# Thresholds of a planned instruction order, chosen by stretch, in an attention and MLP block

## The chip, the cores and the metric

The kernel runs on one core of one Trainium2 chip. The metric is the device time of one execution in microseconds; lower is better. The kernel before was timed in three runs: 2409.73, 2412.84 and 2415.67 us, a median of 2412.84. One more execution was taken with the hardware profiler on, and all rows of the profile come from that one.

The names of the engines are those of the profile: PE is TensorE's matmul, PEld its weight load, DVE VectorE, ACT ScalarE, POOL GpSimd and SP the engine that issues most transfers.

## The reference

A transformer block in f32 for 2048 rows of 576 features: layer norm with scale and shift from a condition vector, attention with 32 heads of 18 features, then a second norm and an MLP of width 4608.

```python
mod = (_silu(c) @ w_mod).reshape(c.shape[0], 6, 1, -1)
sa, ca, ga, sb, cb, gb = ...                       # the six parts of mod
h = _layernorm(x) * (1 + ca) + sa
qkv = (h @ wqkv).reshape(B, S, 3, 32, 18) ...
scores = einsum("bhqd,bhkd->bhqk", q, k) * 18 ** -0.5
o = einsum("bhqk,bhkd->bhqd", softmax(scores), v)
x = x + ga * (o @ wo)
h = _layernorm(x) * (1 + cb) + sb
out = x + gb * (silu(h @ w1) @ w2)
```

## The kernel before

**Tiling.** Queries are cut into four blocks of 512 (`NQB`), heads into eight groups of four (`NQUAD`), so there are 32 units of work for the attention. Keys are cut into 16 tiles of 128. Operands of the projections and of the MLP are split into a high and a low part in the type f32r, and a product is three passes of TensorE over those parts.

**Row scores and scores.** For each unit the kernel first needs the largest score of each query row, so that the exponential doesn't overflow. `slot_a` computes the scores with queries on the partitions (tile `psa`, L802) and takes the row maximum of each 512 on VectorE (`mx`, L804). Forty steps later (`LEAD`), `slot_b` computes the same scores with keys on the partitions (tile `psb`, L852), with the maximum already subtracted, and ScalarE writes the exponential (`pt`, L854). One value of the counter `now` is one `slot_a` and one `slot_b`; two values are one step of row scores. There are 2128 values of `now`; the first 80 are worked off in the first part, before the planned loop starts. The exponentials of a key tile for four heads are ready after four values of `now`, and then `run_pv` multiplies one or more key tiles with the values (tile `psv`, L889): four matmuls a key tile, side by side in four column strips of 32.

**Filling.** Between these, TensorE works off a list of other work (`Filler`): first the query and key projections that are still missing (`qk_one`, L591, full height of 128 rows), then, once the list is empty, the pools for the MLP are opened (`open_mlp`) and the list holds, for the block of queries that has just ended (`post`), the output projection (`psp`), the second norm, the transposes (`h_T`) and the MLP (`mlp1`, `mlp2`; tile `ps`, L486). While those run, the scores of the next block run beside them. After the last block, nothing but its own `post` is left (L480). Scores and most of the MLP use two halves of 64 rows side by side, which the planner calls mode "half"; values are mode "values"; matmuls over all 128 rows are mode "full".

**The planner.** The order of TensorE's instructions is written out in Python when the kernel is built. `Plan` holds a clock `t`, in ns, and what it believes of VectorE and ScalarE: a queue of operations for each with durations (`TMAX` 605 for a row maximum, `TEXP` 495 for an exponential) and rings of PSUM banks that come free when the operation that reads them is done. `Plan.work` moves the clock on by the price of a piece of TensorE work and adds a charge where the mode changes. The prices are `TS` (one value of `now`), `TV` (one key tile of values), `MMC` and `MMH` (a step of 512 or 288 columns of the filling work) and `TX` (a change of mode).

**The choice.** The loop at the end of `tile_adaln_block` picks, at each turn, one of three things: scores ("s"), a piece of the filling work ("f") or values ("v"); where none is possible, the planner's clock moves on by 20 ns with no instruction issued. `scores` says that the banks for one more step are free by the planner's clock and that an exponential's tile is free; `n` counts the key tiles whose exponentials are ready; `ahead` says how many values of `now` the scores are ahead of the pace at which the filling work would be finished in time; `plan.backlog("V")` is the work that waits for VectorE. Nine numbers decide between them:

- `AHEAD`: how far scores may run ahead of the filling work, and filling work ahead of scores
- `KEEP` and `NEAR`: after `open_mlp`, filling work goes first while it is less than `KEEP` values behind the scores' pace and the next point at which it must wait is at most `NEAR` ns off
- `LOADED`: before `open_mlp`, values go first if VectorE has at least so many ns of backlog for each key tile that is ready
- `LOADED2` and `NEXT`: before `open_mlp`, when TensorE is not in mode "half", filling work goes first if VectorE has at least `LOADED2` ns of backlog and the filling work is not more than `NEXT` values ahead
- `STAND`: how long the planner stands before it takes fewer key tiles than it would like
- `PVMAX` and `PVMIN`: the number of ready key tiles that go at once whatever else is possible, and the number that go (after `open_mlp`) before scores where no filling work can start

Before the change each of the nine is one constant for the whole kernel. Row maxima are read by VectorE alone, and banks of `psa` form a ring of three, so where VectorE is behind, the next `psa` matmul stands in TensorE's queue, and all that is queued behind it with it.

The order of the other engines' instructions is the order in which the Python code issues them; a few transfers and conversions are tied to a place in TensorE's order by `after_pe`. The first part (`start_tasks`) has its own planner with its own durations.

Of the kernel before, what the change touches and what calls it, by code (L numbers as in the profile page):

```python
# [57 lines left out]
REST = (16, 8, 0, 0)  # L58
LP = 8000
PB = 9  # L60
PVMAX, PVMIN = 5, 3
EACH, LAND, STORE = (1500, 2000), 5000, 4000
QKB = 3
GS = 2
# [2 lines left out]
GQ = (range(0, 4), range(4, 8), range(8, 11), range(11, 14))  # L67
G2 = [range(i, i + 3) for i in range(0, 24, 3)]
GP = [range(i, i + 2) for i in range(0, 28, 2)]
MMC = 231  # L70
MMH = 133

TS, TV, TX, TL, TR = 231, 906, 95, 430, 60
TMAX, TEXP = 605, 495
TLAT = {"A": 100, "V": 85}
AHEAD = 12
KEEP = 6
NEAR = 500
LOADED = 900
LOADED2 = 900  # L80
NEXT = 8
STAND = 0


def head_rows(h):
# [14 lines left out]
class Plan:  # L100
# [11 lines left out]
    def work(self, cost, mode="half"):  # L112

        if mode != self.mode:
            cost += 2 * TX if mode == "half" else TX
            self.mode = mode
        self.t += cost

# [222 lines left out]
def tile_adaln_block(ctx: ExitStack, tc: tile.TileContext, x, wqkv, wo, w1, w2, c, wfirst, wcol, out):  # L341
# [85 lines left out]
    half = {"at": 0}  # L427
# [82 lines left out]
    full = wqp.tile([P, P], F32, name="full", bufs=1)  # L510
# [74 lines left out]
    def qk_one(which, m, n, w, part):  # L585
        if part == 0:
            qk_ps[0] = psF.tile([P, 512], F32, tag="f", name="psqk")
            qk_ps[1] = plan.take("f")
        for i in GQ[part]:
            kt, a, b = PASS[i]  # L590
            mm(qk_ps[0], lhsT=w[b][:, kt, :], rhs=(hTl if a else hTh)[:, kt, n * 512:(n + 1) * 512], start=(i == 0), stop=(i == 13))  # L591
        if part == len(GQ) - 1:

            hl, tmp = qk_hi(qk_ps[0]), qk_ps["t"].tile([P, 512], F32, name="qt")
            nc.scalar.activation(tmp, qk_ps[0], AF.Copy)
            nc.gpsimd.tensor_tensor(hl[:, 1], tmp, f(hl)[:, 0], op=ALU.subtract)
            qk_store(which, m, n, hl, (0, 1))
            chain([("A", 600), ("A", 600)], plan.t + 200, None, qk_ps[1])
# [31 lines left out]
    def add_qk(steps):  # L630
# [7 lines left out]
        for i, (which, m, pairs) in enumerate(steps):  # L638
            for n in sum(pairs, ()):
                names = [("qkx"[which], m, n)]  # L640
                for p in range(len(GQ)):
                    fill.add(MMC * len(GQ[p]), lambda i=i, which=which, m=m, n=n, p=p: qk_one(which, m, n, qk_w[i], p), name=names, need=bank_need if p == 0 else None, mode="full")
                    if p == 0 and asked:
# [310 lines left out]
    def post(b):  # L954
# [26 lines left out]
        def proj(j, part):  # L981
            if part == 0:
                def ops(g, i):
                    kt, a, w = PASS[i]
                    return (c["tl"] if a else c["th"])[:, kt, j * P:(j + 1) * P], c["wo", kt][:, 1 - w, g * HH:(g + 1) * HH]

                settle(*[("wo", kt) for kt in range(KT)])
                c["pp"] = Pair([bank("psp", psA)[:, :HH] for _ in range(2)], ops, 14, not state["tail"])
            for s in GP[part]:
                c["pp"].step(s)  # L990
            if part == len(GP) - 1:
                for g in range(2):
                    add_x1(j, g, c["pp"].ps[g])
                    plan.op("AV"[g == 0], plan.t + 200, 440, c["pp"].release[g])
# [63 lines left out]
        for j in range(NST):  # L1058
            rest(REST[j])
            steps_ = dict(zip((1, 4, 8, 11), ln_steps(j - 1))) if j else {}  # L1060
            for part in range(len(GP)):
                fl.add(MMH * len(GP[part]), lambda j=j, part=part: proj(j, part), need={0: pair_need if j else o_need, len(GP) // 2: half_need}.get(part))
                if part in steps_:
# [32 lines left out]
        def mlp1(i, part):  # L1096
            if part == 0:
                def ops(g, k):
                    if k == 14:
                        return c["w1", i + g][:, 0, 4 * P:], c["h2"]  # L1100
                    kt, a, w = PASS[k]
                    return c["w1", i + g][:, 1 - w, kt * P:(kt + 1) * P], (c["hl"] if a else c["hh"])[:, kt, :]

                settle(("w1", i), ("w1", i + 1))
                c["p1"] = Pair([bank("ps1", psA) for _ in range(2)], ops, 14, not state["tail"], short=not last)
            for s in GR[not last][part]:
                c["p1"].step(s)
            if part < NG - 1:
                return
            us = c["p1"].ps  # L1110
            if not state["tail"]:

                us = [etmp(), etmp()]
                nc.scalar.activation(us[0], c["p1"].ps[0], AF.Copy)
                nc.vector.tensor_copy(us[1], c["p1"].ps[1])
                c["gs"] = []
                for n in range(2):
                    chain([(("A", 600), ("V", 690))[n], ("A", 630), ("V", 690), ("A", 630)], plan.t + 200, c["p1"].release[n], lambda at: c["gs"].append(at + 1600))
            for g_ in range(2):
                u, t = us[g_], etmp()  # L1120
                nc.scalar.activation(t, u, AF.Tanh, scale=0.5)  # L1121
                nc.vector.scalar_tensor_tensor(t, t, 1.0, u, op0=ALU.add, op1=ALU.mult)  # L1122
                g = pool.tile([P, 2, QB], F32R, tag="g", name="g", bufs=GB)
                nc.scalar.activation(g[:, 0, :], t, AF.Copy)  # L1124
                (nc.vector if last else nc.gpsimd).tensor_tensor(g[:, 1, :], t, f(g[:, 0, :]), op=ALU.subtract)  # L1125
                c["g", i + g_] = g
# [38 lines left out]
        def w_at(n, *loads):  # L1165

            for at, load, i in loads:
                if at == n and i < NFT:
                    fl.add(0, lambda load=load, i=i: load(i))

        def add_mlp1(i, *loads):

            for part in range(NG):
                fl.add(MMC * len(GR[not last][part]), lambda part=part: mlp1(i, part), need={0: pair_need, NG // 2: half_need}.get(part))
                w_at(part, *loads)

        def add_mlp2(i0, add, *loads):
            for j in range(NST):
                for part in range(len(G2)):
                    add(MMH * len(G2[part]), lambda j=j, part=part: mlp2(i0, j, part), None, {0: pair_need, len(G2) // 2: half_need}.get(part))  # L1180
                    w_at(j * len(G2) + part, *loads)
# [375 lines left out]
    now = 2 * LEAD  # L1557
    fill.pace(now, NQUAD * 64 - END0)
    stood = 0
    while now < 2 * (total + LEAD) or pend or later:  # L1560
        plan.advance()
        if "p" not in mp and fill.pos == len(fill.items):
            open_mlp()
            prefetch(0)
        state["now"] = now
        run_later()
        serve()
        fill.free()
        more = now < 2 * (total + LEAD)
        n = kts_ready()  # L1570
        room = state["p"] + (now % 2 == 0) <= len(pts)
        scores = more and room and plan.is_ready(plan.when("b")) and (now // 2 >= total or plan.is_ready(plan.when("a")))
        work = fill.pos < len(fill.items)
        target = fill.target() if work else now + AHEAD - 1
        ahead = now - target
        busy = work and fill.ready()
        if n >= PVMAX or n and more and not room and (ahead < 0 or not busy):
            do = "v"
        elif "p" not in mp:

            if busy and plan.mode != "half" and ahead > -NEXT and plan.backlog("V") >= LOADED2:
                do = "f"
            elif scores and ahead < AHEAD:
                do = "s"
            elif n and plan.backlog("V") >= LOADED * n:
                do = "v"
            elif busy and ahead > -AHEAD:
                do = "f"
            elif scores:
                do = "s"  # L1590
            elif n and stood >= STAND:
                do = "v"
            else:
                do = None
        elif busy and (ahead >= 0 or ahead > -KEEP and fill.rest() <= NEAR):
            do = "f"
        elif n >= PVMIN and not busy:
            do = "v"
        elif scores and ahead < AHEAD:
            do = "s"  # L1600
        elif busy and ahead > -AHEAD:
            do = "f"
        elif n >= PVMIN or n and stood >= STAND:
            do = "v"
        else:
            do = None
        stood = 0 if do else stood + 20
        if not do:
            if not more and not pend:
                run_later(2)  # L1610
                state["now"] += 1
                now += 1
            plan.t += 20
            continue
        if do == "v":
            run_later(1)
            run_pv(n)
        elif do == "f":
            fill.one()
        else:  # L1620
            sa, j = divmod(now, 2)
            plan.work(TS)
            if sa < total:
                slot_a(sa, j)
            slot_b(sa - LEAD, j)
            now += 1
            plan.advance()
# [50 lines left out]
```

## Time and profile before

| what | before |
|---|---|
| median of three runs | 2412.84 us |
| profiled execution, its time | 2407.57 us |
| profiled execution, its span | 2405.8 us |
| TensorE busy | 2323.4 us, 97% |
| VectorE busy | 1775.2 us, 74% |
| ScalarE busy | 1482.1 us, 62% |
| granted TensorE clock, mean | 0.992 |

The span runs from the first to the last instruction of the program; the execution's own time is 1.8 us longer. A row of the profile's fifth part or of a list of groups has the line in the kernel, the engine, the operation, the tile written and the tiles read, the shapes and the count, then the busy time, the mean of one in ns and the idle time of the engine just before them with what ended it. A row of waits has who waited for whom, then the sum in us, the number of times and the longest. A row of a table by stretches has a stretch, its length and for each engine the busy time and the count, then the granted clock. A row of the timeline, or of the chain of waits in order of time, has a start and a length in us and then what ran.

### The profile page before, as it was taken

The page shows a single profiled execution, that of the slowest core. Times are in us where ns is not written, and L with a number is a line of the kernel's source. Part 1 is how long each engine was busy: PE and PEld are TensorE (multiplying, and loading weights), DVE is VectorE, ACT ScalarE, POOL GpSimd, SP SyncE. Part 2 cuts the span into 40 slices and gives each one's busy share as a digit, 9 for nine tenths or more (in the row PEclk, how much of TensorE's full clock was granted, in tenths as well). Part 3 has the DMA queues.
Part 4 walks back from the last instruction along what each step waited for, and adds up shares of the span by engine and source line. Part 5 has one row for each costly group of instructions (what it writes and reads, how often), then busy time and mean ns, then how long its engine had stood idle before and what let it go on. Part 6 is the DMA issues. An engine that isn't in the chain of part 4 may idle for free.

```text
span 2405.8 us, 52151 instructions
## 1 busy us (share of the span) xinstructions
PE 2323.4 (97%) x19844; PEld 1596.2 (66%) x19844; DVE 1775.2 (74%) x3109; ACT 1482.1 (62%) x2734; POOL 637.5 (26%) x769
## 2 busy tenths in 40 slices
PE   6999999998999999998999999999999999989999
PEld 4874444434567766775676777766677777678998
DVE  8768989887878888886887888887877787144333
ACT  5247777775667776675776777775676677722121
POOL 5201011104746676663311111122211111110000
PEclk9999999999999999999999999999999999999999
DMA  7555556445556666665655445554545554336563
GB/s 254 163 173 173 168 170 182 150 159 157 195 191 206 213 223 208 221 220 180 216 172 175 164 164 191 170 181 139 188 160 167 189 166 163 120 113 225 203 206 118
DMA packets 201474, 433.02 MB, mean 180 GB/s; under 512 B 31362, under 2 KB 67618, under 8 KB 201226
## 3 DMA queue, kind: packets, MB, share of 16 engines
q1 hardware_dynamic: 201226, 429.68, 54.5%
q8 instruction: 159, 2.61, 0.5%
q14 instruction: 89, 0.73, 0.1%
HBM read 338.54 MB, written 86.33 MB: 177 GB/s over the span
## 4 chain that ended last, share of the span: by engine, by line
PE 84%; DVE 7%; DMA 4%; ACT 3%; POOL 2%; issue 1%; SPq 0%; ACTq 0%; POOLq 0%; DVEq 0%
PE ps L486 25%; PE psv L889 18%; PE psa L802 13%; PE ps L480 10%; PE psb L852 8%; PE psqk L591 3%; DVE mx L804 3%; PE psp L486 2%; PE psv L486 2%; DMA raw<-in_w 1%; ACT pt L854 1%; PE psqk L486 1%; PE psv L1350 1%; PE psqk L1350 1%; PE psp L480 1%
## 5 line engine op out<-in xcount | busy, mean ns | idle before, releaser
L804 DVE TENSOR_REDUCE mx<-psa 128x1 f32<-128x512 f32 x2048 | 1319.0, 683 | 310.9 <-PE psb L852 161.8
L854 ACT ACTIVATE pt<-psb 128x512 f32<-128x512 f32 x2048 | 1131.5, 598 | 503.1 <-PE psb L852 305.8
L852 PE MATMUL psb<-qt,kb 56*128 56x512 f32 x2048 | 750.1, 423 | 10.7 <-ACT pt L854 9.7
L802 PE MATMUL psa<-ka,qt 54*128 54x512 f32 x2016 | 698.2, 415 | 9.5 <-DVE mx L804 8.0
L802 PEld LDWEIGHTS psa<-ka,qt 54*128 54x128 f32 x2016 | 335.2, 186 | 298.7 <-DVE mx L804 202.0
L889 PE MATMUL psv<-pt,vt 128*32 128x512 f32 x4096 | 513.5, 604 | 2.3 <-ACT ov L893 1.7
L486 PE MATMUL ps<-w2t,g 64*128 64x288 f32 x4992 | 410.5, 294 | 7.7 <-POOL w2t L693 3.9
L486 PEld LDWEIGHTS ps<-w2t,g 64*128 64x128 f32 x4992 | 382.7, 186 | 43.0 <-DVE mx L804 10.1
L852 PEld LDWEIGHTS psb<-qt,kb 56*128 56x128 f32 x2048 | 352.4, 185 | 53.6 <-ACT pt L854 38.4
L486 PE MATMUL ps<-hh,w1t 64*128 64x512 f32 x1944 | 371.6, 395 | 6.8 <-POOL w1t L696 3.1
L486 PEld LDWEIGHTS ps<-hh,w1t 64*128 64x128 f32 x1944 | 220.3, 186 | 44.9 <-DVE mx L804 7.5
L889 PEld LDWEIGHTS psv<-pt,vt 128*32 128x32 f32 x4096 | 99.5, 109 | 215.8 <-issue 208.0
L1125 POOL TENSOR_TENSOR g<-etmp,g 128x512 fp32r<-128x512 f32 x108 | 137.8, 1297 | 392.3 <-ACT g L1124 334.6
L1003 POOL TENSOR_TENSOR x<-x,gt 128x288 f32<-128x288 f32 x116 | 93.6, 807 | 416.9 <-ACT gt L1002 416.9
L486 PE MATMUL ps<-hl,w1t 64*128 64x512 f32 x864 | 198.0, 393 | 0.5 <-POOL hl L413 0.5
L999 DVE TENSOR_TENSOR x<-ps,x 128x288 f32<-128x288 f32 x184 | 83.8, 456 | 124.8 <-PE ps L480 77.1
L480 PE MATMUL ps<-w2t,g 128*128 128x288 f32 x960 | 133.5, 299 | 7.4 <-ACT g L1124 5.9
L480 PEld LDWEIGHTS ps<-w2t,g 128*128 128x128 f32 x960 | 131.1, 191 | 9.9 <-ACT g L1124 6.3
L486 PEld LDWEIGHTS ps<-hl,w1t 64*128 64x128 f32 x864 | 105.3, 186 | 10.8 <-POOL hl L413 0.9
L1121 ACT ACTIVATE eq<-ps 128x512 f32<-128x512 f32 x36 | 21.6, 600 | 146.3 <-PE ps L480 146.3
L480 PE MATMUL ps<-hh,w1t 128*128 128x512 f32 x360 | 106.9, 390 | 0.5 <-DVE hh L415 0.5
L1122 DVE SCALAR_TENSOR_TENSOR etmp<-etmp 128x512 f32<-128x512 f32 x108 | 76.6, 744 | 23.4 <-ACT etmp L1121 23.2
(146 smaller groups left out, 2084.4 us busy)
## 6 DMA issues: line engine op xcount, KB each, us to landing
w1t<-w1s SPq DMA_DIRECT2D x108, 640.0 KB
w2t<-w2s SPq DMA_DIRECT2D x108, 576.0 KB
kb<-kscr SPq DMA_DIRECT2D x512, 108.0 KB
ka<-kscr SPq DMA_DIRECT2D x504, 108.0 KB
w1s<-w1t SPq DMA_DIRECT2D x36, 640.0 KB
w2s<-w2t SPq DMA_DIRECT2D x36, 576.0 KB
vt<-vscr SPq DMA_DIRECT2D x32, 608.0 KB
qt<-qscr SPq DMA_DIRECT2D x128, 108.0 KB
```

The source lines that it names most:

```text
L480: mm(self.ps[late], lhsT=lhsT, rhs=rhs, start=(i == 0), stop=(i == self.n - 1))
L486: done = mm(self.ps[g], lhsT=lhsT[rows], rhs=rhs[rows], start=(s == 0), stop=(s == self.end))
L591: mm(qk_ps[0], lhsT=w[b][:, kt, :], rhs=(hTl if a else hTh)[:, kt, n * 512:(n + 1) * 512], start=(i == 0), stop=(i == 13))
L802: mm(ps, lhsT=t["q"][64 * j:64 * j + 54, hp, stt * P:(stt + 1) * P], rhs=t["a" if ("a", kc, hp) in t else "b", kc, hp][64 * j:64 * j + 54, ...
L804: return lambda: nc.vector.tensor_reduce(t["mx"][:, 2 * j + hp, stt, kc:kc + 1], ps, axis=AX.X, op=ALU.max)
L852: state["pe"] = mm(ps, lhsT=t["b", kt // 4, hp][64 * e:64 * e + 56, kt % 4 * P:(kt % 4 + 1) * P], rhs=t["q"][64 * e:64 * e + 56, hp, :], s ...
L854: nc.scalar.activation(t["P"][kt, hp][:, e, :], ps, AF.Exp, scale=SCALE)
L889: mm(t["ps"][32 * h:32 * h + 32, :], lhsT=t["v"][:, c0:c0 + 32], rhs=t["P"][kt, h // 2][:, h % 2, :], start=(kt == 0), stop=(kt == NKT - 1 ...
L999: nc.vector.tensor_add(c["x1"][j][:, hs], ps, c["x1"][j][:, hs])
L1003: nc.gpsimd.tensor_add(c["x1"][j][:, hs], c["x1"][j][:, hs], t)
L1122: nc.vector.scalar_tensor_tensor(t, t, 1.0, u, op0=ALU.add, op1=ALU.mult)
L1125: (nc.vector if last else nc.gpsimd).tensor_tensor(g[:, 1, :], t, f(g[:, 0, :]), op=ALU.subtract)
```

## The change

Three things change, all of them in the planner. The nine constants become the fields of a rule, and there are thirteen rules, "a" to "m"; "a" holds the nine numbers of before. A table, one letter for each six values of `now` (three steps of row scores), names the rule that the loop reads at each turn; beyond its 285 letters the last one holds. The prices of TensorE's work change (`MMC`, `MMH`, `TS`, `TV`, `TX`), and a change into mode "full" is charged twice `TX`, as one into mode "half" already was. No instruction's operands, no tile, no pool and no transfer is edited.

```diff
-PVMAX, PVMIN = 5, 3
+WAYS = {
+    "a": (12, 6, 500, 900, 900, 8, 0, 5, 3),
+    "b": (12, 6, 500, 1500, 900, 8, 0, 5, 2),
+    "c": (12, 6, 500, 600, 600, 8, 0, 5, 4),
+    "d": (12, 9, 500, 900, 600, 8, 100, 5, 3),
+    "e": (12, 3, 500, 900, 1300, 8, 200, 5, 3),
+    "f": (12, 6, 800, 900, 900, 2, 0, 5, 3),
+    "g": (18, 6, 500, 1500, 600, 8, 0, 5, 3),
+    "h": (18, 9, 800, 600, 1300, 2, 0, 5, 3),
+    "i": (12, 9, 500, 1500, 1300, 8, 100, 5, 2),
+    "j": (8, 6, 250, 900, 900, 4, 0, 4, 3),
+    "k": (24, 12, 500, 1800, 900, 8, 200, 5, 4),
+    "l": (12, 6, 500, 300, 900, 8, 0, 3, 1),
+    "m": (12, 6, 1200, 900, 300, 12, 300, 5, 4),
+}
+SPAN = 6
+TABLE = (
+    "aaaaaaaaaaaaaaakaaaaaaaacaagiaaaaaaaaakaaaaaaaaaaaaaaaaakaaaaaaaaaaecaaaaaaaaaaaaaaaaaaabaaaaaaaaaad"
+    "aggaaaggaaaaaaaaaaaaaaaaaaaaaaaaaaaaaaaaaaaaaaaaaaaaaaaaaaaaaaaaaaaaaaaaaaaaaaaaaaaaaaaaaeaaaamd"
+    "afaaaaaaaaaaaaaaaaaafaaaaacaaaaamaaaaaaaaaaaaaaaaaaaaaaaaaaaaaaaaaaafmalaaaafammfaada"
+)
...
-MMC = 231
-MMH = 133
-
-TS, TV, TX, TL, TR = 231, 906, 95, 430, 60
+MMC = 228
+MMH = 131
+
+TS, TV, TX, TL, TR = 229, 862, 112, 430, 60
...
-AHEAD = 12
-KEEP = 6
-NEAR = 500
-LOADED = 900
-LOADED2 = 900
-NEXT = 8
-STAND = 0
...
     def work(self, cost, mode="half"):
 
         if mode != self.mode:
-            cost += 2 * TX if mode == "half" else TX
+            cost += 2 * TX if mode in ("half", "full") else TX
             self.mode = mode
         self.t += cost
...
     while now < 2 * (total + LEAD) or pend or later:
+        AHEAD, KEEP, NEAR, LOADED, LOADED2, NEXT, STAND, PVMAX, PVMIN = WAYS[TABLE[min(now // SPAN, len(TABLE) - 1)]]
         plan.advance()
```

More of the change, by code (lines that the diff above doesn't have):

```diff
@@ L60 @@
 PB = 9
-PVMAX, PVMIN = 5, 3
+WAYS = {
[13 rows of a table added]
+}
+SPAN = 6
+TABLE = (
+    "aaaaaaaaaaaaaaakaaaaaaaacaagiaaaaaaaaakaaaaaaaaaaaaaaaaakaaaaaaaaaaecaaaaaaaaaaaaaaaaaaabaaaaaaaaaad"
+    "aggaaaggaaaaaaaaaaaaaaaaaaaaaaaaaaaaaaaaaaaaaaaaaaaaaaaaaaaaaaaaaaaaaaaaaaaaaaaaaaaaaaaaaaaaaeaaaamd"
+    "afaaaaaaaaaaaaaaaaaafaaaaacaaaaamaaaaaaaaaaaaaaaaaaaaaaaaaaaaaaaaaaafmalaaaafammfaada"
+)
 EACH, LAND, STORE = (1500, 2000), 5000, 4000
```

## The prediction

> **What bounds the kernel now.** I read the page first, then busy time by stretches, then waits, then single switches in the timeline.
>
> ```profile
> span 2405.8 us, 52151 instructions
> PE 2323.4 (97%) x19844; PEld 1596.2 (66%) x19844; DVE 1775.2 (74%) x3109; ACT 1482.1 (62%) x2734; POOL 637.5 (26%) x769
> PE 84%; DVE 7%; DMA 4%; ACT 3%; POOL 2%; issue 1%; SPq 0%; ACTq 0%; POOLq 0%; DVEq 0%
> L852 PE MATMUL psb<-qt,kb 56*128 56x512 f32 x2048 | 750.1, 423 | 10.7 <-ACT pt L854 9.7
> ```
>
> TensorE has 97% of the span and 84% of the chain that ended last. The change adds and removes no instruction, so it can move only two things: the time in which TensorE waits, and the number of switches between its kinds of work. The busy share hides part of both, because the ends of matmuls are modelled. The L852 row also gives a ruler: one such matmul is one step of `now`, which starts at 80, so the n-th of the 2048 is step 80 + n, and six steps are one letter of the table.
>
> ```profile
> core 0: us, PE busy (x) PEld busy (x) DVE busy (x) ACT busy (x) POOL busy (x), PEclk, DMA share, GB/s
> 300.00:400.00 100.00, 99.40 (x604) 41.77 (x596) 88.07 (x157) 75.59 (x150) 12.00 (x9) 1.00 0.56 168
> 500.00:580.00 80.00, 74.59 (x441) 30.13 (x440) 66.50 (x116) 57.67 (x109) 25.81 (x36) 1.00 0.62 193
> 580.00:620.00 40.00, 35.31 (x321) 23.42 (x321) 28.05 (x68) 16.81 (x32) 13.82 (x23) 0.91 0.25 80
> 620.00:700.00 80.00, 72.00 (x583) 45.92 (x583) 60.34 (x100) 51.97 (x94) 53.71 (x71) 0.96 0.65 215
> 1100.00:1200.00 100.00, 91.41 (x881) 63.00 (x883) 75.67 (x148) 60.27 (x110) 33.04 (x39) 0.97 0.57 190
> 1200.00:1600.00 400.00, 399.54 (x3972) 289.79 (x3969) 324.38 (x542) 285.48 (x526) 65.23 (x63) 1.00 0.51 170
> 1600.00:1740.00 140.00, 134.84 (x1255) 89.13 (x1254) 113.26 (x211) 92.77 (x173) 34.01 (x36) 0.99 0.55 180
> ```
>
> Three regimes show. In the first (about 142 to 545 us) DVE is at 88% and TensorE looks full but is not. Where one block of queries gives way to the next (the rows 500 to 700, 1100 to 1200 and 1600 to 1740) TensorE stands 5.41 + 4.69 + 8.00 + 8.59 + 5.16 = 31.9 us. Between, as in 1200 to 1600, it stands 0.5 us of 400. The tail after the last score reads no table entry.
>
> ```profile
> PEld psa L802 <- DVE mx L804: 202.7, 285, 2.1
> ```
>
> What TensorE meets is mostly the row maximum on VectorE that has not yet freed a score bank: 285 times.
>
> **What a switch costs.** TensorE's own rows, in order of start:
>
> ```profile
> 408.86 0.40 PE L591 MATMUL psqk<-hTh,wqh 128*128 128x512 f32 x1
> 409.09 0.39 PE L591 MATMUL psqk<-hTh,wql 128*128 128x512 f32 x1
> 409.41 0.50 PE L802 MATMUL psa<-ka,qt 54*128 54x512 f32 x1
> 409.75 0.40 PE L802 MATMUL psa<-ka,qt 54*128 54x512 f32 x1
> 410.08 1.06 PE L889 MATMUL psv<-pt,vt 128*32 128x512 f32 x8
> 411.07 0.50 PE L802 MATMUL psa<-ka,qt 54*128 54x512 f32 x1
> ```
>
> Start to start a pass of 512 columns takes 0.23 us (408.86 to 409.09). From a projection to a score it is 0.32, so 0.09 for the switch; from a score into values 0.33, so 0.10. In the chain of waits, runs of one and three key tiles of values take this long until the next kind:
>
> ```profile
> 1118.00 1.00 PE psv L889 x8
> 1184.75 2.71 PE psv L889 x24
> ```
>
> A key tile is (2.71 - 1.00) / 2 = 0.855, so leaving costs 0.14 and a visit to values 0.24 in all. A visit to the projections I take at 0.18, twice the 0.09, since the trace shows its two sides alike.
>
> **The change part by part.** First the planner's clock. Before, any visit costs 95 + 190 = 285 ns in switches; after, a visit to values costs 112 + 224 = 336 and one to full-height work 224 + 224 = 448, because entering "full" is now charged twice too. A key tile falls from 906 to 862, a score step from 231 to 229, a pass from 231 to 228, a half-width one from 133 to 131. I check both clocks against 300 to 500 us, in the first regime:
>
> ```profile
> L804 DVE TENSOR_REDUCE mx<-psa 128x1 f32<-128x512 f32 x252 | 159.2, 682 | 23.6 <-PE psb L852 16.5 <-PE psa L802 5.9
> L889 PE MATMUL psv<-pt,vt 128*32 128x512 f32 x504 | 67.1, 605 | 0.0
> L591 PE MATMUL psqk<-hTh,wqh 128*128 128x512 f32 x62 | 25.7, 414 | 0.0
> L591 PE MATMUL psqk<-hTh,wql 128*128 128x512 f32 x61 | 25.0, 411 | 0.0
> L591 PE MATMUL psqk<-hTl,wqh 128*128 128x512 f32 x49 | 21.9, 447 | 0.0
> ...
> 299.53 1.06 PE L889 MATMUL psv<-pt,vt 128*32 128x512 f32 x8
> 301.43 0.50 PE L591 MATMUL psqk<-hTl,wqh 128*128 128x512 f32 x1
> 497.78 1.06 PE L889 MATMUL psv<-pt,vt 128*32 128x512 f32 x8
> 499.99 0.50 PE L591 MATMUL psqk<-hTh,wqh 128*128 128x512 f32 x1
> ```
>
> The last four rows are the first and last of the 63 runs of values, every one of a single key tile (504 / 8 = 63), and of the 53 visits to full-height work. With 252 score steps, 172 passes and 20 small pieces that the planner books at 0.2 us, its clock before is 252 x 0.231 + 63 x (0.906 + 0.285) + 172 x 0.231 + 4 + 53 x 0.285 = 192 us. After, it is 252 x 0.229 + 63 x (0.862 + 0.336) + 172 x 0.228 + 4 + 53 x 0.448 = 200 us. The chip took 200. At the measured prices the same work is 252 x 0.23 + 63 x (0.855 + 0.24) + 172 x 0.23 + 4 + 53 x 0.18 = 180 us. So TensorE waits about 20 us in 200 here, and the new clock agrees with the chip by booking that waiting as switches.
>
> [...]
>
> What this does: a pending maximum is judged by that clock. In a visit to the projections it now moves 0.16 us further, so more score steps are thought ready when they are asked, and the order fits the pace that the chip has. If waits then shrink, the clock overshoots and brings some back. That limits the gain, so of the 403 x 20 / 200 = 40 us of waiting between 142 and 545 I take a tenth for the clock, 4 us. The bounds are a half (20 us gained) and, the other way, the visits that can be added: 24 projections of four parts and 20 pieces make 116 visits at most, against 53 in 200 of 403 us or some 107 in all, so 9 x 0.18 = 2 us lost.
>
> Now the middle, 1200 to 1600 us:
>
> ```profile
> L804 DVE TENSOR_REDUCE mx<-psa 128x1 f32<-128x512 f32 x414 | 268.8, 684 | 62.3 <-PE psb L852 38.1 <-PE psa L802 21.5
> L486 PE MATMUL ps<-w2t,g 64*128 64x288 f32 x1512 | 121.4, 292 | 0.0
> L486 PE MATMUL ps<-hh,w1t 64*128 64x512 f32 x540 | 101.6, 393 | 0.0
> L889 PE MATMUL psv<-pt,vt 128*32 128x512 f32 x824 | 98.8, 598 | 0.0
> L486 PE MATMUL ps<-hl,w1t 64*128 64x512 f32 x240 | 54.1, 391 | 0.0
> L486 PE MATMUL ps<-h,w1t 64*128 64x512 f32 x30 | 6.6, 390 | 0.0
> ...
> 1208.91 2.78 PE L889 MATMUL psv<-pt,vt 128*32 128x512 f32 x24
> 1595.96 1.92 PE L889 MATMUL psv<-pt,vt 128*32 128x512 f32 x16
> ```
>
> These two are the first and last of 53 rows of values, so 103 key tiles in runs of 1.9. Two records are one planned step: 756 half-width and 405 full-width. The clock before is 414 x 0.231 + 103 x 0.906 + 53 x 0.285 + 756 x 0.133 + 405 x 0.231 = 398 us; after it is 94.8 + 88.8 + 17.8 + 99.0 + 92.3 = 393; the chip took 400. Here the new clock is worse by 5 us. At measured prices (0.133 kept for half-width) the work is 95.2 + 88.1 + 12.7 + 100.5 + 93.2 = 390, so 10 us of waiting and 13 of switches are all there is. Only three changed letters fall in 1316 to 1392 us. I put the three middles (700 to 1100, 1200 to 1600, 1740 to 2120) at 0, between -8 and +10.
>
> Then the table. Of 285 letters 256 are "a", the rule of before; the first 13 are never read, and after step 1710 (about 1709 us) the last "a" holds. By the ruler the 29 others lie: nine at 165 to 515 us, 17 where blocks change (five at 564 to 628, four at 1154 to 1212, eight at 1595 to 1703), three in the middle. The nine of the first regime hold 54 steps, some 46 us with 4.6 of waiting. "b", "g", "i" and "k" ask for 1500 or 1800 ns of backlog ahead of values, and single runs can only merge there, 0.24 us each: I take 1 us. The 17 at the blocks' ends meet the 31.9 us in which TensorE stands. They let fill work run further ahead ("g" 18 steps), count a fill as urgent earlier (NEAR 800 or 1200), or hold values back (STAND). Part of that standing is transfers and the norm's chain, which no order removes, so I take a quarter, 8 us, between 0 and two thirds, 21.
>
> Sum: 4 + 0 + 1 + 8 = 13 us off the profiled execution's 2407.57 (span 2405.8 and 1.8 around it), so 2394.6 there. That execution is 5.3 us under the median of the runs, so against 2412.84 I say 2400.
>
> The granted clock falls to 0.91, 0.96 and 0.97 in the rows 580 to 620, 620 to 700 and 1100 to 1200. [...]
>
> **The rivals.** *One order for another, no change.* For it: the middles are 1180 of the 2407 us and, judged by 1200 to 1600, stand almost nowhere, and 90% of the letters are the old ones. Against: 40 and 31.9 us of waiting lie just where the letters or the clock act. Gains at the blocks' ends are then lost in the middle: 2412.84 within 6 us, about 2411. Nearly the same comes out if the letters have no effect at all and the clock's 4 us alone is left, 2409.
>
> *Shorter runs of values in the middle, slower.* There the new clock runs 5 us in 393 behind the old one, and so further behind the chip. Banks look occupied for longer, fewer scores look ready, and the planner, having nothing else, takes values as soon as one key tile stands. Runs fall from 1.9 toward the single tiles of the first regime. It decides when the mean is under 1.8. At 1.5, the 309 key tiles of the middles (3 x 103) make 206 runs instead of 163: 43 x 0.24 = 10 us, so 2423. Against it: the test for fill stands ahead of that for values, and fill is seldom short there.
>
> **How the numbers follow.** The forecast has 0.56, no change 0.22 (both of its forms), slower 0.22. What a measurement here tells from no change is 0.3%, so 2405.6 to 2420.1. The low end of the range is both gains near their bounds, 20 + 21 = 41 us, 2372; the high end the slower rival at its price, 2424. The forecast's own range is 2385 to 2405.
>
> **What would show it.** Right: less standing in the five rows at the blocks' ends, fewer than 285 waits of score loads on the maximum, single runs of values merged in the first regime, and the stretch from 300 to 500 us holding more than 252 score steps. Wrong: the middle's runs of values shorter than 1.9, or the standing merely moved into 700 to 1100 and 1740 to 2120.

## The result, and the profile after

The changed kernel takes 2385.07 us (median of four runs, 2384.48 to 2385.90) against 2414.26 us for the kernel before (four runs, 2409.73 to 2416.41). The ratio is 0.9884, with a 95% interval from 0.9872 to 0.9896: 1.16% faster. The medians are 29 us apart, where 13 were forecast. The two profiled executions are 22.4 us apart (spans 2405.8 and 2383.4). The rest of the 29 lies in how a single execution stands to its median: the profiled one of before ran some 7 us under its median, the one of after at its own.

The head of the page of the changed kernel (its lines stand 13 lower than those of before):

```profile
span 2383.4 us, 52135 instructions
PE 2311.3 (97%) x19844; PEld 1578.9 (66%) x19844; DVE 1786.6 (75%) x3109; ACT 1491.4 (63%) x2734; POOL 638.8 (27%) x769
PE 84%; DVE 7%; DMA 3%; POOL 2%; ACT 2%; issue 1%; SPq 0%; DVEq 0%; ACTq 0%; POOLq 0%
```

The number of TensorE's instructions is the same, 19844, and so is its share of the chain. Only the order is another. Here are the stretch from 300 to 500 us and then the stretches that answer to the prediction's table, at nearly the same values of `now` and so some microseconds earlier:

```profile
core 0: us, PE busy (x) PEld busy (x) DVE busy (x) ACT busy (x) POOL busy (x), PEclk, DMA share, GB/s
300.00:500.00 200.00, 198.71 (x1220) 85.00 (x1218) 181.14 (x327) 154.65 (x304) 24.37 (x18) 1.00 0.53 165
497.00:577.00 80.00, 75.50 (x452) 31.15 (x450) 67.59 (x118) 59.44 (x112) 28.43 (x39) 1.00 0.60 198
577.00:614.00 37.00, 34.33 (x330) 23.37 (x331) 28.36 (x68) 17.81 (x35) 13.77 (x22) 0.95 0.25 80
614.00:694.00 80.00, 69.21 (x574) 43.86 (x576) 59.13 (x99) 50.16 (x93) 54.28 (x71) 0.94 0.63 216
1090.00:1188.00 98.00, 92.51 (x864) 62.47 (x867) 77.35 (x148) 59.13 (x109) 31.03 (x36) 0.95 0.55 187
1188.00:1592.00 404.00, 403.46 (x4014) 286.30 (x4007) 329.27 (x547) 291.88 (x532) 65.55 (x63) 1.00 0.52 170
1592.00:1727.00 135.00, 132.58 (x1270) 90.24 (x1268) 113.16 (x211) 93.85 (x173) 35.00 (x37) 1.00 0.54 186
```

Where blocks change, TensorE stands 4.50 + 2.67 + 10.79 + 5.49 + 2.42 = 25.9 us, 6 less than before, though the third of the five rows has 2.8 more (10.79 against 8.00). The middle still stands 0.5. In 300 to 500 us the row maxima, one for each score step, have become 259 where they were 252 (a row of the list of groups for that stretch):

```profile
L817 DVE TENSOR_REDUCE mx<-psa 128x1 f32<-128x512 f32 x259 | 163.9, 683 | 18.5 <-PE psb L865 15.1 <-PE psa L815 1.9
```

Standing alone doesn't show where 22.4 us came from, because a TensorE that the profile shows busy hides waiting: in 300 to 500 us of the kernel before it is busy for 198.48 us, and the prediction counts 180 us of bare work there. So I took the records of TensorE's matmuls in both traces and counted, between the same values of `now`, the length less the bare work at the prediction's prices (0.23 us a score step or pass, 0.133 a half-width step, 0.855 a key tile) and less the visits (0.24 to values, 0.18 to full-height work). What is left is **waiting**:

| values of `now` | what runs there | before | new prices, "a" alone | changed kernel |
|---|---|---|---|---|
| 80 to 592 | first stage | 54.2 | 52.3 | 51.9 |
| 592 to 720 | end of block 0 | 37.7 | 39.3 | 34.3 |
| 720 to 1104 | middle | 18.3 | 16.0 | 15.9 |
| 1104 to 1232 | end of block 1 | 21.3 | 20.2 | 21.0 |
| 1232 to 1680 | middle | 15.4 | 18.4 | 16.8 |
| 1680 to 1744 | end of block 2 | 12.6 | 7.8 | 6.8 |
| 1744 to the last score | middle | 17.7 | 14.1 | 14.0 |
| after the last score | tail | 17.5 | 14.9 | 14.7 |
| sum | | 194.8 | 183.1 | 175.4 |
| visits, whole kernel | | 97.9 | 96.1 | 93.8 |

Waiting fell by 19.4 us and visits by 4.1, and the loop began 1.2 us later, 22.3 in all. How far a single row can be trusted shows in the run "early" below, in which TensorE has the changed kernel's order up to value 1157: counted alike, the two differ by 3.5 us at the end of block 0 (34.3 and 37.8) and by 0.5 at most in the rows on either side of it. Differences of that size at the blocks' ends aren't read.

### The profile page after: what moved, and what is told of

It reads as the page before. It is cut to its first block, busy times and chain, and to the rows that moved or that the text cites. A ratio compares the mean times of both kernels' runs of the same rounds, so it can differ in the third digit from the quotient of the medians.

```text
span 2383.4 us, 52135 instructions
## 1 busy us (share of the span) xinstructions
PE 2311.3 (97%) x19844; PEld 1578.9 (66%) x19844; DVE 1786.6 (75%) x3109; ACT 1491.4 (63%) x2734; POOL 638.8 (27%) x769
## 4 chain that ended last, share of the span: by engine, by line
PE 84%; DVE 7%; DMA 3%; POOL 2%; ACT 2%; issue 1%; SPq 0%; DVEq 0%; ACTq 0%; POOLq 0%
PE ps L499 24%; PE psv L902 18%; PE psa L815 13%; PE ps L493 10%; PE psb L865 8%; PE psqk L604 4%; DVE mx L817 3%; PE psv L499 2%; PE psp L499 1%; PE psv L1363 1%; PE psqk L499 1%; DMA raw<-in_w 1%; PE psqk L1363 1%; DMA qt<-qscr 1%; ACT pt L867 1%
## 5 line engine op out<-in xcount | busy, mean ns | idle before, releaser
L867 ACT ACTIVATE pt<-psb 128x512 f32<-128x512 f32 x2048 | 1143.3, 598 | 472.2 <-PE psb L865 293.8
L815 PE MATMUL psa<-ka,qt 54*128 54x512 f32 x2016 | 724.9, 416 | 9.2 <-DVE mx L817 7.7
L499 PE MATMUL ps<-hh,w1t 64*128 64x512 f32 x1944 | 364.4, 395 | 10.2 <-POOL w1t L708 9.2
L499 PEld LDWEIGHTS ps<-hh,w1t 64*128 64x128 f32 x1944 | 202.2, 187 | 52.3 <-POOL w1t L708 10.1
L499 PE MATMUL ps<-hl,w1t 64*128 64x512 f32 x864 | 184.0, 393 | 0.0
L499 PEld LDWEIGHTS ps<-hl,w1t 64*128 64x128 f32 x864 | 92.6, 187 | 13.9
```

The source lines that it names most:

```text
L499: done = mm(self.ps[g], lhsT=lhsT[rows], rhs=rhs[rows], start=(s == 0), stop=(s == self.end))
L815: mm(ps, lhsT=t["q"][64 * j:64 * j + 54, hp, stt * P:(stt + 1) * P], rhs=t["a" if ("a", kc, hp) in t else "b", kc, hp][64 * j:64 * j + 54, ...
L867: nc.scalar.activation(t["P"][kt, hp][:, e, :], ps, AF.Exp, scale=SCALE)
```

## The experiments

Each is an edit of the changed kernel and was timed in rounds beside the kernel before on the same chip. Runs of different sets weren't timed side by side: the kernel before had medians of 2411.57, 2411.69 and 2412.62 us in three sets and 2414.26 with the changed kernel, so a difference of medians across sets can be off by 2 or 3 us. Where a diff gives a table, it gives it as a rule in short; the kernels have the letters written out.

**The new prices alone, and the table alone.** The first has the table

```diff
-TABLE = ( ... )   # 29 letters other than a
+TABLE = "a" * 285
```

> The new prices of the planner's clock with a table that holds the letter a alone, so the thresholds of before everywhere. Theory A (the repriced clock made most of the 29 us): at most 2396 us, 18 us or more under the kernel before. Theory B (the letters at the ends of the blocks made most): 2405 to 2412 us. Theory C (any new order falls within some 10 us of the old one, and the letters are the choice among such orders that came out best): between 2400 and 2412, and no stretch that explains it alone. The prediction's own terms gave 4 us of 13 to the clock, a share of 0.3, which here would be 9 us: 2405.

It took 2394.61 us, ratio 0.9932 (0.9918 to 0.9947). The second keeps the table and takes back the prices:

```diff
-MMC = 228
-MMH = 131
+MMC = 231
+MMH = 133
-TS, TV, TX, TL, TR = 229, 862, 112, 430, 60
+TS, TV, TX, TL, TR = 231, 906, 95, 430, 60
-            cost += 2 * TX if mode in ("half", "full") else TX
+            cost += 2 * TX if mode == "half" else TX
```

> The table and the rules as in the changed kernel, with the prices of before (TS 231, TV 906, TX 95, MMC 231, MMH 133, and one charge for full). Theory A: within 8 us of the kernel before. Theory B: 18 us or more under it, at most 2396 us, with the gain in the stretches from 560 to 630 us and from 1595 to 1745 us. Theory C: since the letters were found for another clock, anywhere within 10 us of the kernel before.

It took 2407.60 us, ratio 0.9978 (0.9969 to 0.9988). So the prices alone make 16 us, the table alone 5, and the table on top of the prices 9.5 by the medians, 11.6 by the ratios. Theory A's figures are met, but not in the place that the prediction gave the clock: the column above puts only 2 us of the prices' gain into the first stage and most at the end of block 2 and behind it.

**One charge for full height**, once with the table and once with "a" everywhere:

```diff
-            cost += 2 * TX if mode in ("half", "full") else TX
+            cost += 2 * TX if mode == "half" else TX
```

> The changed kernel, with a change into full height charged once (112 ns) rather than twice, as before. If the match of the clock with the chip in the stretch 300 to 500 us makes the first stage's gain, the stage before the first block's end gets some 4 us longer again, 2389 us in all; if the double charge matters nowhere but in the first stage and there little, within 3 us of the changed kernel, 2385.

2388.39 us, ratio 0.9907 (0.9891 to 0.9924).

> Letter a everywhere and the new prices, but a change into full height charged once, so that a visit to the projections costs the planner 336 ns, not 448. Against the run with all new prices and letter a (2394.6). If the double charge makes the gain of the first stage, that stage (which was 420 us long there, and 416 with all new prices but that of values) gets 3 to 7 us longer and the whole 2398 to 2402. If it is all prices together by chance, no direction is foretold: 2392 to 2410.

2398.36 us, ratio 0.9945 (0.9925 to 0.9966). Twice the double charge is worth 3 to 4 us (2388.39 - 2385.07 and 2398.36 - 2394.61); the intervals overlap, so it is the agreement of the two that speaks, not either. The place is the first stage: its waiting is 51.9 us with the double charge and 56.4 without under the table, 52.3 and 54.5 under "a". Under "a" the stage got 1.9 us longer (406.6 against 404.7), less than the 3 to 7 that were expected.

**Prices at the bare work**, with letter "a" everywhere.

```diff
-MMC = 228
-MMH = 131
+MMC = 230
+MMH = 133
-TS, TV, TX, TL, TR = 229, 862, 112, 430, 60
+TS, TV, TX, TL, TR = 230, 857, 112, 430, 60
-            cost += 2 * TX if mode in ("half", "full") else TX
+            cost += TX
```

> Letter a everywhere and prices at what the trace shows for bare work: a key tile 857, a score step and a pass 230, a half-width step 133, and 112 ns once for any change of mode, so 224 for a visit of either kind. The prediction's step was that the clock fits the chip by booking the waiting as switches. By it, a clock without the waiting runs ahead of nothing and behind the chip by some 10% in the first stage: slower than the new prices by 8 us or more, 2402 to 2415. If prices near the true ones are what makes a good order: 2395 or less.

2418.26 us, ratio 1.0027 (1.0015 to 1.0040): slower than before, slower than the range expected, and 24 us slower than the new prices with the same letters. The row maxima of 300 to 500 us, first with the new prices and "a", then with the bare ones:

```profile
L817 DVE TENSOR_REDUCE mx<-psa 128x1 f32<-128x512 f32 x254 | 160.3, 682 | 22.1 <-PE psb L865 18.6 <-PE psa L815 2.5
```

```profile
L817 DVE TENSOR_REDUCE mx<-psa 128x1 f32<-128x512 f32 x251 | 159.0, 683 | 24.3 <-PE psb L865 20.8 <-PE psa L815 3.0
```

The first stage ends, at the first matmul of the output projection, at 574.2 and at 587.1 us (the row of the tile `psp`, first and last start):

```profile
L499 PE MATMUL psp<-wo,th x480: 286/292/480, 574.2 to 1669.2; 64*128 64x288 f32 x160
```

```profile
L499 PE MATMUL psp<-wo,th x480: 285/292/438, 587.1 to 1685.4; 64*128 64x288 f32 x160
```

So 12.9 of the 26.9 us between these two profiled executions (spans 2391.8 and 2418.7) are there when the first stage ends. Booking the bare work made a worse order here than booking some of the waiting with it, as the prediction's comparison of the two clocks with 200 us said.

**The price of values apart.** Letter "a", and of the new prices `TV = 862` alone; then all but it (`TV = 906`).

> Letter a everywhere, and of the new prices the one of a key tile of values alone (TV 862 for 906); all others as before. If the time of values is the price that made the new clock's gain in the MLP stages (15 of its 17 us fell there, where values are taken in runs of about two key tiles), at most 2400 us, 12 us or more under the kernel before. If it is the charge for changes of mode, or all of them together by chance, within 6 us of the kernel before.

> Letter a everywhere and all new prices but that of values (TV stays 906). The counterpart of the run with the one price: if values made the gain, within 6 us of the kernel before; if the changes of mode did, at most 2400 us. Both under 2400, or neither, would speak for no single price: then the gain is that of one order among many (theory C).

2411.84 us, ratio 0.9999 (0.9988 to 1.0011), and 2404.77 us, ratio 0.9971 (0.9961 to 0.9981). Neither is under 2400; together they are 2394.61. At the end of block 2, where 12.6 us were waited before, it is 12.9 with the one, 10.9 with the other, 7.8 with both. No single price made it.

**Six clocks, one stage.** The runs with letter "a" everywhere, and the kernel before, differ in their prices alone. For each, the table has what its prices add up to for the prediction's counts of 300 to 500 us, and how long the first stage took (values 80 to 592, from first score to first score in its trace).

| order | clock for the 200 us | first stage, us |
|---|---|---|
| bare prices | 182 | 416.1 |
| `TV` alone new | 189 | 411.2 |
| before | 192 | 407.2 |
| full height charged once | 194 | 406.6 |
| new prices | 200 | 404.7 |
| all new but `TV` | 203 | 401.1 |

The more the clock books, the shorter the stage, in all six. The three orders under the table say the same: 410.8 us at 192 (the table alone), 408.4 at 194 and 402.4 at 200. It isn't noise of an execution: the run "late" below has the TensorE order of the new prices with "a" up to value 1157 and took 404.9, and "early", with that of the changed kernel, 402.1. Orders with the new prices and the letters at other places took 402.1 to 406.5, so the whole span of 15 us is clear of such chances, while a single step of 2 or 3 us in it is not. But 203, more than the chip's 200, is best of all in this stage, so these runs don't show that agreement with the trace is the best point. And the whole kernel with that clock is 10 us slower than with the new prices (2404.77 against 2394.61): the later stages don't follow this rule.

**The letters by place.** New prices, with the letters before entry 160 alone ("early"), then those behind it alone ("late"):

```diff
-TABLE = ( ... )
+TABLE = "".join(c if i < 160 else "a" for i, c in enumerate(TABLE))    # early; i >= 160 for late
```

> New prices, and of the 29 letters only the 14 of the first attention block and its end (up to about 630 us). The letters' gain over the new prices alone was 9.5 us, and the two profiles put about 9 us of it ahead of 650 us. If that is where they act: 2385 to 2389. If an early gain is given back later unless the later letters catch it: 2390 to 2396.

> New prices and only the 15 letters behind 1150 us. If the letters act where they stand and their gains add up, 9.5 us less what the early ones alone save, so 2391 to 2395. If the late letters are worth as much alone, 2385 to 2390 (then the sum would not add up, which speaks for theory C).

2389.46 us, ratio 0.9905 (0.9882 to 0.9927), and 2393.39 us, ratio 0.9925 (0.9906 to 0.9944). Against 2394.61 the early letters save 5 and the late ones 1, against 9.5 for both; with these intervals it can't be told whether the gains add up.

**The letters moved.** The same 29 letters, at two random placings, and the whole table moved by one entry:

```diff
-TABLE = ( ... )
+TABLE = "a" + TABLE[:-1]         # moved by one; the other two: the letters of entries 13 to 284 shuffled
```

> The new prices, and the same 29 letters put at places drawn at random from all that are read. Theory B in its strong form (a letter is good for any stretch like it, or for its place): the gain of the letters is gone and the time is that of the new prices alone, or some us over it. Theory C: the same, with a scatter of some 5 us that has no stretch of its own. If the rules were good wherever they stand, it would be within 5 us of the changed kernel, 2385 to 2390.

> A second random placing of the 29 letters with the new prices; the first was 21 us slower than letter a everywhere. If rules at random places cost as such, 2405 to 2420 again. If the first was an unlucky draw, around 2394, between 2388 and 2402.

> The changed kernel with its table moved by one letter, so that every rule acts six values of the counter, some 5 us, later. If a letter is good for the kind of stretch (the end of a block), most of the 9.5 us that the letters were worth stays: 2385 to 2390. If the letters are good only for the one decision at which they act, they are lost and the time is that of letter a or some us more: 2394 to 2402.

2415.43 us, ratio 1.0020 (1.0007 to 1.0033); 2389.37 us, ratio 0.9912 (0.9893 to 0.9931); and 2399.68 us, ratio 0.9945 (0.9924 to 0.9967). So the letters as rules show no worth that holds apart from their places. A step of 5 us takes the gain away, one random placing costs 21 us, another saves 5. The first random placing waited 10 us more between 1104 and 1232 (30.2 us by the count above, against 20.2 with the letter "a"), and its chain of waits shows part of the reason:

```profile
1198.34 0.93 PE ps L499 x8
1200.27 8.39 DMA w1t<-w1s
1208.71 2.07 PE ps L499 x7
```

TensorE came to the MLP's weights before their transfer had landed, and stood 0.50 and 2.15 us for it (the rows of `ps` at 1206.06 and 1208.71 us in its timeline). In its table by stretches the clock was granted at 0.86 from 1195 to 1220 us:

```profile
1195.00:1220.00 25.00, 22.35 (x160) 14.05 (x158) 15.69 (x25) 14.47 (x27) 2.48 (x2) 0.86 0.64 191
```

With 25 x 0.14 = 3.5 us for the lower clock, an estimate, some 6 of the 10 us are accounted for.

## Why the prediction was right, and where not

**The clock in the first stage: right.** It was to save 4 us by booking the waiting as switches, the letters 1 more by merging single runs of values. The stage became 4.8 us shorter: 2.3 of waiting and 2.5 of visits (to values 127 to 121, to full height 90 to 84, counted from the records). The sum fits better than its parts: 2.5 us came with the prices (407.2 to 404.7) and 2.3 with the letters, which did merge single runs (126 visits to values with the prices alone, 121 with the letters). That the clock acts here is shown by the six clocks above, and the stretch from 300 to 500 us holds more than 252 steps, as foretold. A slip without weight: the 54 steps of the early letters take 43 us at 252 steps in 200 us, not 46.

**The middle at 0: this step failed.** The waiting of the three middles fell by 2.4 - 1.4 + 3.7 = 4.7 us, and what comes after the last score, for which the sum had no term, gave 2.8 more: 7.5 in all. The 4.7 are inside the bounds (8), but the term was set to 0 because the new clock fits 1200 to 1600 us less well, 393 against 400. The fit of the clock's sum over a stretch therefore doesn't decide alone; what does in the middles isn't shown. The rival built on that misfit, shorter runs of values, did not come either. Its ruler was misread: three of the 53 rows are runs that lie across the edge of two windows of the timeline and were counted twice, so there are 50 runs of 2.06 key tiles in 1200 to 1600 us, not 53 of 1.9. In the changed kernel the same values of `now` have 48 runs of 2.17, and 9 of a single tile where there were 15.

**The blocks' ends: the size near, the cause half wrong.** 8 us were forecast there, from the letters. Waiting fell by 3.4 + 0.3 + 5.8 = 9.5, but 4.3 of it (71.6 to 67.3 over the three rows) come with the prices alone, and at the end of block 2 it is 4.8 of 5.8. The letters' share is mostly at the end of block 0, 39.3 to 34.3, and there the same order also gave 37.8, so it lies between 1.5 and 5. That the size came out near is in part luck. One thing the late letters do can be seen. TensorE's rows at the transposes (`psT`) of block 2, before:

```profile
1675.34 0.40 PE L802 MATMUL psa<-ka,qt 54*128 54x512 f32 x1
1675.34 0.39 PE L852 MATMUL psb<-qt,kb 56*128 56x512 f32 x1
1675.58 2.93 PE L486 MATMUL ps<-w2t,g 64*128 64x288 f32 x36
1679.05 1.09 PE L1036 MATMUL psT<-ident,ob 128*128 128x128 f32 x8 [0.54 <-DVE x L999]
1680.58 1.32 PE L1036 MATMUL psT<-ident,ob 128*128 128x128 f32 x8 [0.43 <-ACT etmp L406]
1682.19 0.63 PE L1036 MATMUL psT<-ident,ob 128*128 128x128 f32 x4 [0.29 <-ACT etmp L406]
1682.75 0.50 PE L802 MATMUL psa<-ka,qt 54*128 54x512 f32 x1
...
1688.53 0.50 PE L802 MATMUL psa<-ka,qt 54*128 54x512 f32 x1 [1.34 <-DVE mx L804]
```

and after:

```profile
1667.22 0.49 PE L815 MATMUL psa<-ka,qt 54*128 54x512 f32 x1
1667.22 0.50 PE L865 MATMUL psb<-qt,kb 56*128 56x512 f32 x1
1667.65 1.09 PE L1049 MATMUL psT<-ident,ob 128*128 128x128 f32 x8
1668.68 0.49 PE L815 MATMUL psa<-ka,qt 54*128 54x512 f32 x1
1668.68 0.49 PE L865 MATMUL psb<-qt,kb 56*128 56x512 f32 x1
1669.18 1.32 PE L1049 MATMUL psT<-ident,ob 128*128 128x128 f32 x8
1671.10 0.63 PE L1049 MATMUL psT<-ident,ob 128*128 128x128 f32 x4 [0.59 <-ACT etmp L419]
1671.65 0.50 PE L815 MATMUL psa<-ka,qt 54*128 54x512 f32 x1
```

Before, no score is issued for 7.4 us (1675.34 to 1682.75). VectorE stands for 1.61 and 1.56 us in that time, then is busy without a break from 1684.0 to 1690.8 when the scores come in a burst, and TensorE waits for it (1.34 us at 1688.53). After, scores stand between the transposes and the longest gap is 3.0 us. The new prices with "a" still have such a gap, 8.2 us, and wait only 1.0 us more there than the changed kernel. So this is a small part, and most of that end's 5.8 us came with the prices. By what step they do it, and which price, isn't settled.

**Letters as rules: wrong.** The prediction read them as suited to the blocks' ends. Seven orders with the same prices lie at 0.9884 (the changed kernel), 0.9905, 0.9912, 0.9925, 0.9932, 0.9945 and 1.0020 of the time before; the table gave the lowest of them. "One order for another", given as a rival with no change, describes this part better; its spread was mis-sized, at 6 us, where these seven lie 33 us apart. That the table was chosen among such orders by some measure is an inference from these runs, not shown.

**Signs and the sum.** The standing did not move into the middles: by the table above, waiting fell in the first and the last of them. Fewer than 285 waits of score loads on the maximum was a wrong sign: there are 292, of the same total (a row of the list of waits).

```profile
PEld psa L815 <- DVE mx L817: 201.8, 292, 1.7
```

These are waits of weight loads. They come to 201.8 us, where the matmuls' waiting of every kind comes to 175.4 us by the count above, so by that count not all of them delayed a matmul. The sum, 13 for 22.4 in the traces, is short by the middle (7.5), by visits (4.1 against 1), and by 1.5 at the blocks' ends, less some 2 too many in the first stage and the loop's 1.2 us later begin. The remaining 7 of the 29 us lie in the profiled execution of before, which ran that far under its median. The result, 2385.07 us, is 15 us under the 2400 that was said, and lies within 2385 to 2405 by less than 0.1 us.

**The granted clock**, for which the sum has no term, gave nothing over the three rows that the prediction names: 0.95, 0.94 and 0.95 after, against 0.91, 0.96 and 0.97 before. At one place in block 2's end it did; that is told in the last section.

## What to carry to other kernels

Where an order is planned from prices, the prices that serve best need not be the bare durations. What the clock adds up to over a stretch can be laid beside the trace from one table of counts before anything is run; in the first stage here a clock short of the trace's time made a longer stage, in the middles the fit told nothing. A table of thresholds found by trying is worth what its one order is worth; move it by a step, or change a price, and it has to be found again. Before crediting a rule, time the same rules in other places: here that spread, 33 us, was larger than the whole effect.

## What the runs showed of the hardware

In two traces a lower granted clock stands by gaps of TensorE that are each short, 1.34 us at most in the one, 0.50 and 2.15 us in the other. In the kernel before, a run of two key tiles of values takes 3.50 us at the end of block 2 (in the chain of waits), where it took 1.85 elsewhere, as in the second of these rows:

```profile
1690.69 3.50 PE psv L889 x16
...
1713.11 1.85 PE psv L889 x16
```

The table by stretches has that run and the 3.4 us ahead of it:

```profile
1687.40:1690.80 3.40, 2.03 (x16) 1.15 (x20) 3.40 (x6) 1.10 (x2) 1.53 (x2) 0.97 1.00 402
1690.80:1694.20 3.40, 3.40 (x18) 0.49 (x14) 0.67 (x2) 0.09 (x1) 0.00 (x0) 0.53 0.56 223
```

The granted clock is 0.53 in the 3.4 us that follow 3.4 us in which TensorE was 60% busy (2.03 of 3.40), and the longest gap there was 1.34 us. The other trace is that of the first random placing: in the 25 us that hold the waits of 0.50 and 2.15 us told above, the clock was granted at 0.86. That the gaps brought the clock down isn't shown by two places. The changed kernel has no such stretch at the end of block 2 (1.00 in the row from 1592 to 1727 us), which by the two runs of values above accounts for an estimated 1.65 us (3.50 - 1.85) of the 5.8 saved there.
